# A transformer block on one core: transposes moved to DMA, full-array matmuls at both ends, and a new split of work between ScalarE and VectorE

## The chip, the core and the metric

The kernel runs on one core of one Trainium2 chip. The metric is the device time of one execution in microseconds (us). The core has a matrix engine (TensorE, "PE" in the profile, with its weight loads as "PEld"), VectorE ("DVE"), ScalarE ("ACT"), GpSimd ("POOL") and SyncE ("SP"), which here issues all DMA transfers. Each engine works through its own list of instructions in order and waits on semaphores for the others.

## The reference

2048 rows of width 640 go through layer normalization, attention with 32 heads of width 20, a residual add, a second normalization and a gated feed-forward block of width 1728 with a second residual add. Inputs and output are bf16.

```
xn = (x - mean) / sqrt(var + 1e-5)
q, k, v = split(xn @ wqkv)                      # 32 heads of 20
p = softmax(q @ k.T / sqrt(20));  o = p @ v     # per head, 2048 x 2048
h = x + o @ wo
hn = layernorm(h)
out = h + (gelu(hn @ w_gate) * (hn @ w_up)) @ w_down
```

## The kernel before, in words

**Order of work.** The kernel doesn't issue instructions as it goes. `Sched.op` (line 59) records every operation with an engine, an estimated duration, a latency, a priority, what it reads and writes and which PSUM banks it takes. `Sched.schedule` (92) then simulates all engines with these estimates and writes down an order for each; `emit` (229) puts it out with semaphore waits. So the order on every engine, SP included, is fixed by the planner's estimates: where something takes longer on the chip than planned, everything behind it in that engine's list waits too. Priorities run from P_QK (0, the attention scores) over P_PV (1) and P_EPI (2) to P_BG (3, background). Where the planner sees TensorE idle for too long it adds a filler matmul (`idle`, 1031).

**Prologue** (574 on). For each 128-row tile of x: statistics on VectorE (`ln_stats`, 499: two bn_stats and an aggregation), one reciprocal square root for four tiles (`ln_rsqrt`, 509), the normalization itself on ScalarE or VectorE (`ln_apply`, list LNE), five TensorE transposes into PSUM and one copy of the result to SBUF (`transposes`, 549; the list LNV names the engine of that copy). GpSimd meanwhile clears two padded weight arrays and copies the weights into them with each head padded from 20 to 32 rows (`pad`, 486).

**Projections** (`proj`, 598). Eight groups of four heads. Keys and queries of a group are 128 x 512 blocks. Beside each, the squares are summed by a second matmul: keys give the maximum squared norm (`kmx`, `khalf`), and half of the sum of norms is put into an extra row of the query as a softmax shift. All 128-column matmuls outside of attention are issued as four matmuls of 32 columns (`quarters`, 587), each on its own quarter of the array.

**Attention.** Queries come in seven chunks of 512, 512, 256, 256, 256, 128 and 128 rows (`CHUNKS`), divided into 32 slots of 64 tiles; a tile is 128 keys by 512 columns of scores. The string PATS says for each slot whether units (`unit`, 727) have three and two tiles in turn, or always three. A unit's scores are written to adjacent PSUM banks, and ScalarE takes the exponential of the whole unit at once. In some three-tile units the third tile goes to VectorE, which computes a polynomial exponential (`d_exp`, 695): one pass out of PSUM for each tile and then seven passes over a pair of tiles. The string DS gives the number of pairs in each slot, 95 pairs or 190 tiles in all. The normalized output of a slot is put into `o_nat` by `epilogue` (837).

**After a chunk** (`post`, 870). Each row tile of `o_nat` is transposed (five blocks, `transposes`), multiplied by `wo`, added to a reloaded x, normalized, transposed again, and goes through gate, gelu, up, multiply and down. This is background work that runs beside the attention of the next chunk. For the last chunk (`tail`) there is nothing beside it but what is left of the chunk before.

The planner gives DMA loads a landing time from a formula (line 206).

Of the kernel before, what the change touches and what calls it, by code (L numbers as in the profile page):

```python
# [6 lines left out]
ALU = mybir.AluOpType  # L7
# [11 lines left out]
DMA_RATE = 0.36  # L19
LATE = (0, 1, 2, 3, 4)  # L20
LNE = [{'a': 'act', 'd': 'dve'}[x] for x in 'aaaaaaaadddddddd']
LNV = [{'a': 'act', 'd': 'dve'}[x] for x in 'aaaaaaaaaaaaaaaa']
# [6 lines left out]
MODE_SWITCH = {"pe": 0.1, "act": 1.3}  # L29
# [14 lines left out]
class Op:  # L44
    __slots__ = ("i", "eng", "fns", "dur", "lat", "prio", "deps", "succ", "nd", "ready",
                 "acq", "rel", "group", "sem", "tag", "mode", "start", "fin", "pos", "know", "mb")


class Sched:
# [9 lines left out]
    def op(self, eng, fns, dur, prio, reads=(), writes=(), acq=(), rel=(), after=(), sem=None, lat=None, mode=None, mb=0.0):  # L59
# [4 lines left out]
        o.mb = mb  # L64
        o.tag = writes[0] if writes else None
# [26 lines left out]
    def schedule(self):  # L92
# [20 lines left out]
        dma_free = 0.0  # L113
        qk_left = sum(o.eng == "pe" and o.prio[0] == P_QK for o in ops)
        t = 0.0
        while done < len(ops):
# [4 lines left out]
            for e in ENGINES:  # L121
# [103 lines left out]
                qk_left -= e == "pe" and o.prio[0] == P_QK  # L225
# [74 lines left out]
_cs = (512, 512, 256, 256, 256, 128, 128)  # L300
# [13 lines left out]
ND, NDA = 4, 6  # L314
RSQRT_MAGIC = float(0x5F3759DF)

P_QK, P_PV, P_EPI, P_BG = 0, 1, 2, 3


def bass_sequential_preLN__mha_block__glu_gated_geglu__prompt_kernel(  # L320
# [12 lines left out]
    with ExitStack() as es:  # L333
# [22 lines left out]
        gq = sb("gq", [128, 128])  # L356
# [74 lines left out]
        zb = carve(2 * 512).rearrange("p (i s) -> p i s", i=2)  # L431

# [18 lines left out]
        cst(I("memset", gq[:], 0.0), "gq")  # L451
        for j in range(4):
            cst(I("memset", gq[32 * j:32 * j + 21, 32 * j:32 * j + 1], 1.0), "gq", 1)
        cst(I("memset", wk_pad, 0.0), "wkpm", 2600)
        cst(I("memset", wq_pad, 0.0), "wqpm", 2600)
# [29 lines left out]

        def pad(dst, off, h0, h1, mkey, key, a0, a1):
            src = wqk[:, a0:a1, off + h0 * DH:off + h1 * DH].rearrange("p a (h e) -> p a h e", e=DH)
            e_ops.append(op(POOL, I("tensor_copy", dst[:, a0:a1, h0:h1, 1:21], src),
                            0.1 + (a1 - a0) * (h1 - h0) * DH * 0.0012, P_BG, reads=["wqk", mkey], writes=[key, "pool"]))
# [4 lines left out]
        for dst, off, key in pads:  # L494
            for a in range(NA):
                pad(dst, off, 4, 32, key + "m", key, a, a + 1)


        def ln_stats(src, t, rkeys, prio, after=()):
# [7 lines left out]
            return [a, b]  # L507

# [40 lines left out]
        def transposes(src, rkeys, dst, wkey, banks, prio, evac, after=()):  # L549
            bk = Bank(*banks)  # L550
            key = ("bk", id(bk), sc_id())
            for a in range(NA):
                op("pe", lambda eng, a=a: eng.transpose(  # L553
                    bank16(bk, D)[:, 128 * a:128 * a + 128], src[:, a * 128:(a + 1) * 128], ident[:]),
                   0.056, prio, mode="full", reads=list(rkeys) + ["ident"], writes=[key], acq=[bk] if a == 0 else [],
                   after=tuple(sc.rd.get(wkey, ())) if a == 0 else ())
            v = lambda: bank16(bk, D).rearrange("p (a e) -> p a e", a=NA)
            if evac == "act":
                op("act", lambda eng: eng.activation(dst, v(), ACT.Copy), c_act(D), prio, reads=[key],
                   writes=[wkey], rel=[bk], after=after)  # L560
            else:
                op("dve", lambda eng: eng.tensor_copy(dst, v()), c_dve(D), prio, reads=[key], writes=[wkey],
# [11 lines left out]
        for t0 in range(0, NT, 4):  # L574
            for t in range(t0, t0 + 4):
                ln_stats(x_sb[:, t, :], t, [f"x{t // 4}"], P_EPI)
# [7 lines left out]

        w_readers = []

# [5 lines left out]
        def chain(bk, key, n, steps, reads, prio, acq=True, after=()):  # L592
            for k, (l, r) in enumerate(steps):
                yield op("pe", quarters(lambda: bank(bk, n), l, r, k == 0, k == len(steps) - 1),
                    c_mm(n), prio, mode="col", reads=reads, writes=[key], acq=[bk] if (k == 0 and acq) else [],
                    after=after if k == 0 else ())

        def proj(which, g, c, banks, prio, evac="dve"):
# [28 lines left out]
            gm = gq if which == "k" else gqh  # L627
# [67 lines left out]
        def d_exp(b, tile, prio):  # L695
# [3 lines left out]
            if not first and d_n[1] == 0:  # L699
                d_n[:] = [0, 1]  # L700
# [10 lines left out]
            if h == 0:  # L711
                return
# [356 lines left out]
```

## Time and profile before

| what | value |
|---|---|
| median of 3 runs | 963.77 us (963.38 to 965.76) |
| profiled execution | 966.23 us, span 964.4 us |
| mean granted TensorE clock | 0.996 |
| VectorE busy | 769.8 us (80%) |
| ScalarE busy | 913.5 us (95%) |
| first exponential starts | 38.67 us into the span |
| last exponentials end | about 924.6 us |

Times in the profile count from the span's start. In a group's row, the columns are the line, engine, operation, output <- input with shapes, count, then total busy us and mean ns of one, then the idle time of the engine just before such instructions and what ended it. The line is often 341, a helper that builds most instructions, so groups are told apart by their tiles. In a row of the timeline, the columns are start, length, engine, line, operation and count, and in brackets the idle time before it. In the chain of waits each piece has a start, a length, an engine and a tile.

### The profile page before, as it was taken

To read this page: it belongs to the slowest core of one execution; us is meant where nothing else is said; L and a number is where in the kernel's file an instruction comes from. 1 tells how busy PE (TensorE), PEld (TensorE's weight loads), DVE (VectorE), ACT (ScalarE), POOL (GpSimd) and SP (SyncE) were. 2 spreads that over 40 slices of the span, in tenths; PEclk is the share of its full clock that TensorE was granted. 3 is DMA by queue.
4 is the path that set the end of the run, shared out by engine and by line. 5 is a ranking of instruction groups with operands and counts; after the bars stand their busy time and mean duration, and the time that the engine had idled before them with its cause. 6 is when DMAs were issued, how large, how long until landed. Compare 5 with 4: busy or idle time off the path is not lost.

```text
span 964.4 us, 35452 instructions
## 1 busy us (share of the span) xinstructions
PE 896.8 (93%) x16302; PEld 395.0 (41%) x16302; DVE 769.8 (80%) x1644; ACT 913.5 (95%) x872; POOL 19.9 (2%) x42
## 2 busy tenths in 40 slices
PE   5999999999999999899999999999999999899976
PEld 3533332222332332323343333444554455566655
DVE  8658857998988788699778888889889877988451
ACT  5799999999999999999999999999999999999961
POOL 8000000000000000000000000000000000000000
PEclk9999999999999999999999999999999999999999
DMA  7000000000000520000010000010000000000000
GB/s 246 3 30 1 2 2 1 2 1 1 2 1 1 211 68 1 2 1 9 16 36 2 2 2 2 9 30 23 2 3 10 23 3 17 17 3 4 12 10 18
DMA packets 11764, 20.04 MB, mean 21 GB/s; under 512 B 544, under 2 KB 9696, under 8 KB 11616
## 3 DMA queue, kind: packets, MB, share of 16 engines
q1 hardware_dynamic: 11616, 17.78, 5.5%
q8 instruction: 128, 2.10, 0.9%
q14 instruction: 20, 0.16, 0.1%
HBM read 15.16 MB, written 2.62 MB: 18 GB/s over the span
## 4 chain that ended last, share of the span: by engine, by line
ACT 75%; PE 16%; DVE 7%; DMA 1%; issue 1%; DVEq 0%
ACT pts L341 44%; ACT rege L341 30%; PE ps L589 9%; PE ps L341 6%; DVE qt_all L341 2%; DVE rege L341 2%; DVE stats L341 1%; DMA rege<-in_A_x_dram 1%; ACT L341 1%; PE ps L553 1%; DVE mv L341 0%; PE ps L850 0%; DVE rege L971 0%; DVE rege L959 0%; DVE osb L341 0%
## 5 line engine op out<-in xcount | busy, mean ns | idle before, releaser
L341 ACT ACTIVATE pts<-ps 128x1024 bf16<-128x1024 f32 (+1 forms) x491 | 560.4, 1352 | 7.9 <-PE ps L341 7.6
L341 ACT ACTIVATE rege<-ps 128x1024 bf16<-128x1024 f32 (+1 forms) x307 | 365.6, 1351 | 0.2
L341 PE MATMUL ps<-qt_all,kt_all 32*128 32x256 bf16 (+2 forms) x3584 | 312.9, 288 | 32.5 <-ACT pts L341 12.9
L341 PEld LDWEIGHTS ps<-qt_all,kt_all 32*128 32x128 bf16 x3584 | 97.6, 92 | 276.8 <-ACT pts L341 126.1
L589 PE MATMUL ps<-rege,regw 128*32 128x256 bf16 (+2 forms) x3780 | 173.2, 289 | 14.3 <-issue 8.2
L341 PE MATMUL ps<-pts,v_all 128*21 128x256 bf16 (+2 forms) x1998 | 162.4, 292 | 1.7 <-DVE osb L341 0.9
L589 PE MATMUL ps<-regw 128*32 128x512 bf16 (+1 forms) x1920 | 133.9, 354 | 1.4 <-DVE qt_all L640 0.8
L341 PE MATMUL ps<-rege,v_all 128*21 128x256 bf16 (+2 forms) x1438 | 129.2, 292 | 0.1
L589 PEld LDWEIGHTS ps<-rege,regw 128*32 128x32 bf16 x3780 | 85.0, 96 | 46.6 <-issue 24.2
L341 DVE TENSOR_TENSOR rege<-rege 128x1024 bf16<-128x1024 bf16 (+1 forms) x149 | 101.6, 684 | 1.5
L589 PE MATMUL ps<-regw,rege 128*32 128x320 bf16 (+1 forms) x1792 | 94.4, 305 | 1.7 <-DVE rege L971 0.7
L341 DVE TENSOR_SCALAR rege<-ps 128x512 int16<-128x512 f32 x114 | 77.9, 684 | 18.1 <-PE ps L341 17.7
L341 DVE TENSOR_SCALAR rege<-rege 128x1024 int16<-128x1024 int16 (+1 forms) x206 | 84.5, 419 | 2.0
L341 PEld LDWEIGHTS ps<-pts,v_all 128*21 128x21 bf16 x1998 | 48.1, 90 | 64.7 <-issue 55.4
L341 DVE TENSOR_TENSOR qt_all<-qt_all 128x1024 bf16<-128x1024 bf16 (+1 forms) x97 | 66.3, 683 | 1.0
L589 PEld LDWEIGHTS ps<-regw 128*32 128x32 bf16 x1920 | 45.8, 95 | 40.3 <-issue 14.4
L341 DVE TENSOR_SCALAR qt_all<-ps 128x512 int16<-128x512 f32 x76 | 52.1, 686 | 12.2 <-PE ps L341 11.6
L341 DVE TENSOR_SCALAR qt_all<-qt_all 128x1024 bf16<-128x1024 int16 (+1 forms) x135 | 56.2, 420 | 1.5
L341 PEld LDWEIGHTS ps<-rege,v_all 128*21 128x21 bf16 x1438 | 40.2, 90 | 39.1 <-issue 33.9
L589 PEld LDWEIGHTS ps<-regw,rege 128*32 128x32 bf16 (+1 forms) x1792 | 44.6, 96 | 27.7 <-issue 15.0
L341 PE MATMUL ps<-wo,gq 128*21 128x256 bf16 x331 | 55.1, 273 | 0.0
L971 DVE TENSOR_TENSOR rege<-rege,ps 128x512 bf16<-128x512 bf16 (+2 forms) x53 | 35.9, 678 | 16.7 <-PE ps L589 16.5
(82 smaller groups left out, 690.4 us busy)
## 6 DMA issues: line engine op xcount, KB each, us to landing
rege<-in_A_x_dram SPq DMA_DIRECT2D x6, 640.0 KB, 5.8
out_dram<-rege SPq DMA_DIRECT2D x16, 160.0 KB, 1.8
regw<-in_B_w_gate_dram SPq DMA_DIRECT2D x1, 2160.0 KB, 8.7
regw<-in_B_w_up_dram SPq DMA_DIRECT2D x1, 2160.0 KB, 14.1
regw<-in_B_w_down_dram SPq DMA_DIRECT2D x1, 2080.0 KB, 19.3
rege<-in_A_wqkv_dram SPq DMA_DIRECT2D x1, 1600.0 KB, 11.3
rege<-in_A_x_dram SPq DMA_DIRECT2D x3, 320.0 KB, 3.4
regw<-in_A_wqkv_dram SPq DMA_DIRECT2D x1, 800.0 KB, 12.9
```

The source lines that it names most:

```text
L341: return lambda eng: getattr(eng, method)(*args, **kwargs)
L553: op("pe", lambda eng, a=a: eng.transpose(bank16(bk, D)[:, 128 * a:128 * a + 128], src[:, a * 128:(a + 1) * 128], ident[:]), 0.056, prio, ...
L589: return [lambda eng, j=j: eng.matmul(out()[j:j + 32], l[:, j:j + 32], r, start=start, stop=stop, tile_position=(0, j), skip_group_check=T ...
L971: hdone.append(op("dve", lambda eng, bu=bu, fv=fv, m=m, w_=w_: eng.tensor_tensor(fv, fv, bank(bu, w_)[0:m, :], ALU.mult), c_dve(w_), p, re ...
```

## The change

- **Transposes.** In `post` of all chunks but the last, both transposes of a row tile become five DMAs each (`dma_start(..., transpose=True)`) issued by SP from SBUF to SBUF, in place of five TensorE transposes and a VectorE copy. For chunks after the first, a block of `o_nat` waits only for the head groups that it holds. The planner counts 0.06 us of SP and 2.6 us of latency for each. In the last chunk the first two blocks of `o_nat` are transposed apart from the other three, still on TensorE.
- **ScalarE and VectorE tiles.** DS now counts single tiles, 209 in all; a slot with an odd number ends with a half-width pass. PATS has six three-tile slots in place of five. From the third chunk on VectorE has seven buffers in place of four.
- **Prologue.** Statistics of five row tiles (list LNS) are computed on ScalarE by two passes with an accumulated sum. Nine of the sixteen copies after the transposes go to VectorE. GpSimd clears only the pad columns, and copies the weights of head groups 1 to 7 after the normalization. The maximum of the squared key norms is taken over 128 columns (the four heads' sums lie on different partitions and are folded by a small matmul). For the first query block the squared norms are added before the key maximum is known.
- **Full-array matmuls.** An operation can carry an alternative (`alt`). Before the first and after the last attention scores, the planner issues one matmul over the full 128 columns (`whole`) in place of four quarters, in the projections, in `post` and for filler matmuls.
- **Smaller ones.** The epilogue of 128-row chunks does one multiply for its four head groups; the last chunk's down projection starts without the last multiply; the planner's table load for ScalarE is 1.55 in place of 1.3 us.

```diff
-PATS = '22222222322222222222332222322322'
-DS = '02204423321344542244444334433422'
+PATS = '22222222322222232222332222222332'
+DS = '06408656668788988888888688668844'
...
+LNS = [{'a': 'act', 'd': 'dve'}[x] for x in 'ddaadddddddaddaa']
+LNE = [{'a': 'act', 'd': 'dve'}[x] for x in 'aaaaaaaaddaddddd']
+LNV = [{'a': 'act', 'd': 'dve'}[x] for x in 'ddddadaaadaaadad']
...
+                if o.alt is not None and (not qk_left or not qk_done):
+                    o.fns, o.mode = o.alt, "full"
...
-        cst(I("memset", wk_pad, 0.0), "wkpm", 2600)
-        cst(I("memset", wq_pad, 0.0), "wqpm", 2600)
+        for w_, key in ((wk_pad, "wkpm"), (wq_pad, "wqpm")):
+            v_ = w_.rearrange("p a h e -> p (a h) e")
+            cst(I("memset", v_[:, :, 0:1], 0.0), key, 160)
+            cst(I("memset", v_[:, :, 21:32], 0.0), key, 1760)
...
+        def ln_stats_act(src, t, rkeys, prio):
+            op("act", I("activation", xn_t[:, t % 2, :], src, ACT.Identity, scale=1.0 / D, accum_out=mv[:, t, 0:1]), 0.65, prio,
+               reads=rkeys, writes=[("mv0", t), ("xnj", t % 2)])
+            op("act", I("activation", xn_t[:, t % 2, :], src, ACT.Square, bias=mv[:, t, 0:1], scale=-1.0, accum_out=mv[:, t, 1:2]),
+               0.65, prio, reads=list(rkeys) + [("mv0", t)], writes=[("mv1", t), ("xnj", t % 2)])
...
+            if DT and dma:
+                aft = tuple(after) + tuple(sc.rd.get(wkey, ()))
+                for a in range(NA):
+                    op("sp", I("dma_start", dst[:, a, :], src[:, a * 128:(a + 1) * 128], transpose=True), 0.06, prio,
+                       reads=rkeys if len(rkeys) < NG or first_ else rkeys[0:(a * 128 + 127) // 80 + 1], writes=[wkey] if a == NA - 1 else [(wkey, a)], sem=f"t{wkey[1]}", lat=2.6, after=aft)
+                return
...
+        def whole(out, l, r, start, stop):
+            return [lambda eng: eng.matmul(out()[0:l.shape[-1]], l, r, start=start, stop=stop, skip_group_check=True)]
...
-                op("dve", lambda eng: eng.tensor_reduce(kmx[:, g, c:c + 1], bank(b2), AX.X, ALU.max), c_dve(512), prio,
+                op("dve", lambda eng: eng.tensor_reduce(kmx[:, g, c:c + 1], bank(b2, 128), AX.X, ALU.max), c_dve(128), prio,
...
-            n = 2 * int(DS[s_])
+            n = int(DS[s_], 16)
...
-                transposes(o_nat[:, tt, :], [("on", g) for g in range(NG)], oT[:, :, ht * 128:(ht + 1) * 128],
-                           ("hnT", ht), banks, P_EPI, ev, after=first)
+                if tail:
+                    transposes(o_nat[:, tt, :], [("on", g) for g in range(4)], oT[:, :, ht * 128:(ht + 1) * 128],
+                               ("oTa", ht), banks, P_EPI, "dve", after=tuple(sc.rd.get(("hnT", ht), ())), al=(0, 1))
+                    transposes(o_nat[:, tt, :], [("on", g) for g in range(NG)], oT[:, :, ht * 128:(ht + 1) * 128],
+                               ("hnT", ht), banks, P_EPI, ev, after=first, al=(2, 3, 4))
+                else:
+                    transposes(o_nat[:, tt, :], [("on", g) for g in range(NG)], oT[:, :, ht * 128:(ht + 1) * 128],
+                               ("hnT", ht), banks, P_EPI, "dve", after=first, dma=True, first_=c == 0)
...
-                           banks, p, ev, after=first)
+                           banks, p, "dve", after=first, dma=not tail)
...
-                           writes=[key], acq=[bk] if f == 0 else [], after=hdone[-2:] if f == 0 else ())
+                           writes=[key], acq=[bk] if f == 0 else [], after=hdone[-4 if tail else -2:][:2] if f == 0 else ())
```

More of the change, by code (lines that the diff above doesn't have):

```diff
@@ L693, in bass_sequential_preLN__mha_block__glu_gated_geglu__prompt_kernel, with d_exp @@
         p_next = [0]
[L695 to L700 removed]
+        def d_exp(b, tile, prio, end):
+            c = slots[tile[0]][0]
+            first = c == 0
+            nd, dvs, dfs, nm_ = ((NDA, dva, dfwa, "a"), (ND, dv, dfw, "b"), (NDC, dvc, dfw, "b"))[min(c, 2)]
+            if d_n[1] != min(c, 2):
+                d_n[:] = [0, min(c, 2)]
             i, h = (d_n[0] // 2) % nd, d_n[0] % 2
```

174 lines of the change are left out of this document (117 added, 57 removed).

## The prediction

> **What bounds the kernel now.** I read the head of the page first, then a table of stages cut where ScalarE's stream of exponentials begins and ends, then the chain of waits.
>
> ```profile
> span 964.4 us, 35452 instructions
> PE 896.8 (93%) x16302; PEld 395.0 (41%) x16302; DVE 769.8 (80%) x1644; ACT 913.5 (95%) x872; POOL 19.9 (2%) x42
> ```
>
> ```profile
> 0.00:38.67 38.67, 28.65 (x444) 17.01 (x444) 31.45 (x98) 22.51 (x36) 19.87 (x42) 1.00 0.45 154
> ...
> 257.30:475.00 217.70, 205.90 (x2526) 68.69 (x2527) 187.04 (x379) 217.64 (x208) 0.00 (x0) 1.00 0.10 34
> 475.00:592.00 117.00, 110.44 (x1869) 45.53 (x1861) 93.03 (x196) 115.05 (x111) 0.00 (x0) 0.99 0.04 11
> ...
> 924.60:964.40 39.80, 27.68 (x1127) 21.17 (x1127) 11.17 (x28) 9.63 (x13) 0.00 (x0) 0.96 0.04 12
> ```
>
> The columns are the stretch, its length, then busy PE, PEld, DVE, ACT, POOL. There are three kernels in one: a prologue of 38.7 us in which no engine is full, 885.9 us of attention in which ScalarE is full (217.64 of 217.70 in query chunk 1), and a tail of 39.8 us with ScalarE almost idle. Each needs its own sum. ScalarE's price of a tile is read from the chain, where its exponentials stand end to end:
>
> ```profile
> 60.42 2.26 ACT rege L341 x2
> ...
> 155.53 2.75 ACT rege L341 x3
> ```
>
> ```profile
> L341 ACT ACTIVATE pts<-ps 128x1024 bf16<-128x1024 f32 x328 | 353.8, 1211 | 0.2
> L341 ACT ACTIVATE pts<-ps 128x1536 bf16<-128x1536 f32 x162 | 263.8, 1641 | 7.7 <-PE ps L341 7.6
> L341 ACT ACTIVATE rege<-ps 128x1024 bf16<-128x1024 f32 x206 | 226.5, 1206 | 0.2
> L341 ACT ACTIVATE rege<-ps 128x1536 bf16<-128x1536 f32 x101 | 163.1, 1647 | 0.0
> ```
>
> Three two-tile exponentials take 2.75 us, so one is 0.917; one of each kind takes 2.26, so a three-tile one is 1.343. (The means of 1211 and 1641 ns overlap their neighbours and are not the price.) Now 534 x 0.917 + 263 x 1.343, and one single tile, make 843.4 us of the 885.9.
>
> **The change, part by part: ScalarE.** Running the two lists PATS and DS through the lines that form units gives 543 two-tile and 251 three-tile exponentials, with 209 tiles on VectorE instead of 190: 543 x 0.917 + 251 x 1.343 = 835.0. That is **-8.4 us**, of it 3.6 in chunk 1 (8 tiles more) and 3.5 in chunk 2 (8 more), as long as nobody makes ScalarE wait.
>
> **VectorE** must carry those tiles.
>
> ```profile
> L341 DVE TENSOR_SCALAR rege<-ps 128x512 int16<-128x512 f32 x114 | 77.9, 684 | 18.1 <-PE ps L341 17.7
> ...
> L631 DVE TENSOR_REDUCE kmx<-ps 128x1 f32<-128x512 f32 x32 | 21.7, 687 | 13.1 <-PE ps L589 13.0
> ...
> L562 DVE COPY rege<-ps 128x640 bf16<-128x640 bf16 x30 | 14.4, 487 | 5.5 <-PE ps L553 5.1
> ```
>
> ```profile
> 436.64 1.20 DVE qt_all L341 x2
> ...
> 442.49 0.33 DVE qt_all L341
> ```
>
> End to end a PSUM read or a bf16 product costs 0.60 and a scalar pass 0.33, so a tile is 0.60 plus half of (4 x 0.33 + 3 x 0.60), 2.2 us. Eight tiles are 17.4. The 30 evacuations of line 562 go (0.49 each, 8 of them per large chunk, 3.9). Chunk 1 becomes 187.0 + 17.4 - 3.9 = 200.5 of 214.1 us, chunk 2 93.0 + 17.4 - 3.9 = 106.5 of 113.5: both 94%. It fits, with little air. The key maxima shrink from 512 to 128 columns, in chunk 0, which has room; the small fold that they need instead is cheaper still. The merged epilogue multiply for the 128-row chunks and the half-width last pair are worth fractions of a microsecond and lie in the same cover; I count them as nothing, and at 94% their loss would cost at most their own time, under 1 us.
>
> **Transposing DMAs.** 15 row tiles x 2 transposes x 5 blocks are 150 PE transposes removed and 150 DMAs put on SP, which issues in order. TensorE's saving is worth nothing in attention, where filler matmuls take its idle time. What counts is lateness: every engine's order is written from a plan, and the plan gives a block 0.06 us of SP and 2.6 us to land, so five land 2.9 us after the first. If they land later, the matmul that reads them blocks TensorE's queue, the scores behind it, and then ScalarE. The trace shows this once already:
>
> ```profile
> 490.44 6.01 DMA rege<-in_A_x_dram
> ```
>
> ```profile
> 499.13 1.45 ACT L341 ACTIVATE pts<-ps 128x1536 bf16<-128x1536 f32 x1 [1.85 <-PE ps L341]
> ```
>
> A reload planned at 4.1 us by the plan's own formula (0.64/0.36 + 1.9 + 0.6 x 0.64) took 6.01, and ScalarE stood still for 1.85 us: lateness passes through almost whole. No transposing DMA is in the trace; the nearest rows are small plain ones.
>
> ```profile
> 750.79 0.39 SPq L341 DMA_DIRECT2D rege<-in_A_x_dram  x1
> 751.22 0.47 SPq L341 DMA_DIRECT2D out_dram<-rege  x1
> ```
>
> ```profile
> out_dram<-rege SPq DMA_DIRECT2D x16, 160.0 KB, 1.8
> ...
> rege<-in_A_x_dram SPq DMA_DIRECT2D x2, 160.0 KB, 2.5
> ```
>
> Let a block take c us of SP or of the queue. The fifth lands at 4c + 1.8, which is 4c - 1.1 beyond the plan. This hurts before the gate matmuls, which wait for the last tile of a chunk, once in each of chunks 0 to 5. Where a chunk has several tiles, each tile's 5c also has to keep up with normalized rows that come about 1.8 us apart (my estimate from chunk 0, four between 337.7 and 343.1): nine tiles come after the first of their chunk, 5c - 1.8 each. The output-side transposes hurt less: all but their last block depend on earlier head groups alone and go out early, except in chunk 0, where the q projections stand between. So the cost is 6 x (4c - 1.1) + 9 x (5c - 1.8). At c = 0.39 it is 4, at 0.47 it is 8, at 0.30 under 2. I take **+8** (c = 0.47, the store). Below nothing it can hardly go: the path that it replaces is hidden, and its freed VectorE time is counted above. SP is also passed by reloads and stores in the same order; a store that waits for its second half holds the transposes behind it, but the next chunk's chain starts later than that store, so I add nothing for it.
>
> The Trainium skill has a price for the operation itself, in "VectorE: DVE Perf Modes", section "The three transpose paths": 1309 ns for a 128x128 bf16 block by the DMA crossbar against 390 ns on TensorE. No run here shows it. Used for c, it would make this term 67 us and the whole change a loss of some 44 us.
>
> **Prologue.**
>
> ```profile
> 2.40 8.80 POOL L341 MEMSET regw<- 128x5120 bf16 x2
> ...
> 9.34 1.89 DVE L341 CAST mv<-mv 128x8 bf16<-128x8 f32 x1
> ...
> 26.59 1.51 DVE L341 TENSOR_SCALAR rege<-rege,mu,rs 128x640 bf16<-128x640 bf16 x4
> ...
> 28.66 2.49 ACT L559 ACTIVATE regw<-ps 128x640 bf16<-128x640 bf16 x4
> ...
> 37.26 0.75 DVE L640 SCALAR_TENSOR_TENSOR qt_all<-ps,khalf,qt_all 128x512 bf16<-128x512 f32 x1
> ...
> 38.67 2.37 ACT L341 ACTIVATE pts<-ps 128x1536 bf16<-128x1536 f32 x2 [3.78 <-PE ps L341]
> 42.24 1.45 ACT L341 ACTIVATE pts<-ps 128x1536 bf16<-128x1536 f32 x1 [1.21 <-PE ps L341]
> ```
>
> ```profile
> L341 DVE BATCH_NORM_STATS2 stats<-rege 128x6 f32<-128x320 bf16 x64 | 28.3, 475 | 1.7 <-DMA rege<-in_A_x_dram 1.4
> ```
>
> VectorE's normalization ends at 28.1 and sets the first exponential. Five tiles' statistics leave it (10 x 0.44 = 4.4). The long cast, which ends as GpSimd's two memsets end (11.2), loses 1.7, since only the pad columns are cleared now. Some seven of the nine evacuations that ScalarE hands over (0.49 each, 3.4) come before the last normalization. Net -2.7. Behind it, four evacuations in a row on ScalarE (2.49) become two on each engine, -1.2; the reduction 0.69 to 0.2 and the final add 0.75 to 0.3, with the squared-norm matmul taken ahead of the maximum, against four small new steps of about 0.15: about -1. ScalarE gets ten passes of about 0.62, mostly in the time before 11.5 in which it had nothing. The ten pad copies for the later head groups, moved behind the normalization, now run beside the key chain. Sum **-5**, between -1 (copies slow the chain) and -8.
>
> **Tail.**
>
> ```profile
> 927.64 0.85 PE L589 MATMUL ps<-rege,regw 128*32 128x128 bf16 x48 [0.63 <-ACT rege L341]
> 928.43 0.45 PE L553 MATMUL ps<-ident,o_nat 128*128 128x128 bf16 x5
> ...
> 935.15 1.02 PE L589 MATMUL ps<-rege,regw 128*32 128x128 bf16 x51 [1.44 <-issue]
> ...
> 943.16 3.20 PE L589 MATMUL ps<-rege,regw 128*32 128x128 bf16 x216
> 947.52 1.97 PE L589 MATMUL ps<-rege,regw 128*32 128x128 bf16 x128 [1.16 <-issue]
> 951.54 1.97 PE L589 MATMUL ps<-rege,regw 128*32 128x128 bf16 x128 [2.05 <-issue]
> 955.29 1.41 PE L589 MATMUL ps<-rege,regw 128*32 128x128 bf16 x68 [1.78 <-issue]
> 957.31 4.32 PE L589 MATMUL ps<-regw,rege 128*32 128x320 bf16 x112 [0.61 <-DVE rege L948]
> ```
>
> ```profile
> 29.16 0.73 PE L553 MATMUL ps<-ident,rege 128*128 128x128 bf16 x10
> ```
>
> Here TensorE stops after bursts of 128 quarter matmuls for about 2 us with nothing that it waits for ("issue"): it seems to run out of instructions. 32 products of 128x128 by 128 columns take 955.29 - 951.54 = 3.75 us, 0.117 each. As one full-array matmul a product costs what a transpose of that size does, (0.73 - 0.45)/5 = 0.056. The last chunk's gate and up (140 products, 943.16 to 956.7 = 13.5 us) become 140 x 0.056 = 8, **-5.5**. Chunk 5's 70 up products, 927.64 to 936.2, become 4, so the last chunk's statistics no longer stand behind their VectorE multiplies, and its down products fit before the gate: of the 18.6 us from 924.6 to 943.16 I let go **-4**. The down products start before the last multiply (0.6, so **-0.5**). Together **-10**; from -5 (only the stalls of the last gate and up go) to -13.
>
> **Sum.** -8.4 - 5 - 10 + 8 = -15.4. The profiled execution took 966.2 us (span 964.4), 2.5 above the median of the three runs, 963.8; carried to the median the forecast is **948**.
>
> **Rivals.** *Everything lands in time* (c at 0.3 or less, or slack that I don't see): the 8 vanish, 940. For it speaks that TensorE has waits of its own to lend; against it, the 1.85 us above. *Transposes too slow, the other sign*: the place is the gate matmul of chunks 0 to 5; the price is the formula; gains of 23.4 are used up at c = 0.67. At c = 0.85 the cost is 36 and the time 976. Against it: plain issues of 0.39 and 0.47; for it: no row shows that a transpose is as cheap as a copy. The page of the Trainium skill named above stands at the far end of this rival. *VectorE becomes the bound in chunks 1 and 2*: if half of the idle 30.7 and 24.0 us there are waits that can't be filled, chunk 1 needs 216 us and chunk 2 118.5, together 7 more: 955.
>
> **How the numbers follow.** Chances: forecast 0.48 (its own range 943 to 956), all in time 0.24, VectorE the bound 0.08, transposes too slow 0.20. A difference of 0.3% (3 us) is about what a measurement can tell. Slower gets the last case, 0.20; within 0.3% gets 0.05 out of the slow end of the others; faster 0.75. The range goes from 936 (all in time, prologue and tail at their better ends) to 976, the slow case at c = 0.85; beyond lies about half of that case and a little below.
>
> **What would show it.** Right: ScalarE at full in attention with exponentials of 835 us; first exponential near 33 to 35; no "issue" gaps of 2 us in the tail, gate and up in 8 to 9 us, tail near 30. In the list of DMAs, transposes with a landing of some 2 to 4 us; at the gate matmuls of each chunk, TensorE waiting for them a microsecond or two, and ScalarE behind it. Wrong: SP busy for 0.7 us or more per block, ScalarE waiting tens of microseconds, or VectorE at 97% and more in chunks 1 and 2.

## The result, and the profile after

The changed kernel takes **1045.07 us** (median of 4 runs, 1044.04 to 1046.15) where the kernel before takes 963.58 beside it: a ratio of 1.0841, with a 95% interval of 1.0817 to 1.0865. The forecast was 948, with 976 as the upper end. It is 81.5 us slower where some 15 us faster were expected.

The head of the page of the changed kernel, with the strips of ScalarE and of TensorE's granted clock:

```profile
span 1043.3 us, 33388 instructions
PE 895.1 (86%) x15135; PEld 387.1 (37%) x15138; DVE 783.8 (75%) x1705; ACT 913.3 (88%) x880; POOL 17.4 (2%) x54
...
ACT  8799999999989579999895799959869799859991
PEclk9999999999989789999997899979979899979999
```

ScalarE and TensorE have as much to do as before (913.5 and 896.8 us there), VectorE 14 us more. But ScalarE's share fell from 95% to 88%, and within attention its strip is down to between 5 and 8 in a dozen slices; the clock's strip falls at most of the same places. The stages say where the time lies. This is the same table of stretches as in the prediction (stretch, length, busy PE, PEld, DVE, ACT, POOL, then the clock), cut at the first and the last exponential:

```profile
0.00:36.22 36.22, 21.58 (x174) 12.44 (x177) 28.28 (x95) 26.73 (x48) 17.39 (x54) 1.00 0.48 164
36.22:1013.66 977.44, 848.34 (x14642) 354.66 (x14641) 744.20 (x1585) 877.85 (x820) 0.00 (x0) 0.94 0.07 19
1013.66:1043.30 29.64, 25.19 (x320) 20.02 (x320) 11.33 (x27) 8.71 (x12) 0.00 (x0) 1.00 0.04 13
```

Against the kernel before (38.67, 885.9 and 39.8 us), the prologue is 2.5 shorter, the tail 10.2 shorter, and attention 91.5 longer. The same cut of attention before:

```profile
38.67:924.58 885.91, 840.48 (x14732) 356.82 (x14731) 727.17 (x1518) 881.35 (x824) 0.00 (x0) 1.00 0.05 15
```

ScalarE was busy for 881.35 of 885.91 there; here it is for 877.85 of 977.44. So ScalarE's own work shrank by 3.5, and its idle time grew from 4.6 to 99.6. That idle time is what has to be explained. In the list of ScalarE's instructions in order of time, these are two of the exponentials that it was late for (start, duration, and in brackets the idle time before it):

```profile
359.05 1.02 ACT L353 ACTIVATE rege<-ps 128x1024 bf16<-128x1024 f32 x1 [9.45 <-PE ps L353]
370.69 1.02 ACT L353 ACTIVATE pts<-ps 128x1024 bf16<-128x1024 f32 x1 [7.84 <-PE ps L353]
```

Both wait for scores from TensorE, at a time when the first chunk's rows are normalized; at 568 and 580 us, with the next chunk's, stand two more of 9.21 and 8.83. What TensorE and VectorE wait for is in the table of waits (us in total, times, longest):

```profile
ACT pts L353 <- PE ps L353: 62.6, 26, 11.3
...
PE ps L636 <- DMA rege<-xn_t: 43.5, 5, 10.9
ACT rege L353 <- PE ps L353: 40.3, 14, 10.9
...
DVE xn_t L353 <- DMA rege<-xn_t: 20.3, 4, 6.0
```

Nearly all of ScalarE's idle time is waiting for scores (62.6 and 40.3 over the whole run). Line 636 is the helper that issues quarter matmuls; those that wait for the transposed normalized rows are the feed-forward's gate matmuls: 43.5 us in only five waits, one in each of chunks 0 to 4, with the scores of line 353 queued behind them. VectorE waits 20.3 us in four waits before it may write normalized rows. The chain of waits of the stretch from 340 to 380 us, which holds the two late exponentials (start, duration, what), shows both ("SPq" is SP's queue, "issue" time in which nothing that the profile shows was waited for):

```profile
343.04 0.28 DVE xn_t L353
...
352.97 1.23 SPq L353
354.20 0.04 issue
354.24 2.42 DMA rege<-xn_t
...
356.69 0.45 DVE xn_t L353
357.13 1.21 DVE qt_all L353 x2
...
358.39 3.41 PE ps L353 x15
...
366.99 2.37 DMA rege<-xn_t
...
369.49 0.62 PE ps L636 x3
```

Between 343 and 366 us the rows of SP alternate like the two shown: a transposing DMA holds it for 1.23 us, with 0.04 to the next, **1.27 us a block**, and the data is there 2.4 us after its issue began. Twenty of them stand one behind the other here (the list of SP's instructions; start, duration, count):

```profile
259.82 26.66 SPq L353 DMA_TRANSPOSE rege<-o_nat  x20
...
342.90 25.32 SPq L353 DMA_TRANSPOSE rege<-xn_t  x20
```

The two late exponentials are now readable. VectorE finished the normalized rows of the second tile at 343.3. `xn_t` has two buffers (its index is `t % 2`), so the third tile may be written only once the first has been transposed out of its buffer, and the fourth only once the second has. VectorE's list shows both waits:

```profile
350.23 0.45 DVE L353 TENSOR_SCALAR xn_t<-rege,mu,rs 128x640 bf16<-128x640 bf16 x1 [4.29 <-DMA rege<-xn_t]
...
356.69 0.45 DVE L353 TENSOR_SCALAR xn_t<-rege,mu,rs 128x640 bf16<-128x640 bf16 x1 [5.68 <-DMA rege<-xn_t]
```

The second tile's last block lands at 356.66. VectorE can't go on in its list until then, the query evacuations `qt_all` that stand behind it start at 357.13, the scores that need them at 358.39, and ScalarE gets its exponential at 359.05, 9.45 us late. Then the last tile's blocks land at 369.36, the gate matmul of line 636 starts at 369.49 with scores behind it, and ScalarE is late again by 7.84.

### The profile page after: what moved, and what is told of

Read it like the earlier page. It is cut to its first block, busy times and chain, and to the rows that moved or that the text cites. A ratio compares the mean times of both kernels' runs of the same rounds, so it can differ in the third digit from the quotient of the medians.

```text
span 1043.3 us, 33388 instructions
## 1 busy us (share of the span) xinstructions
PE 895.1 (86%) x15135; PEld 387.1 (37%) x15138; DVE 783.8 (75%) x1705; ACT 913.3 (88%) x880; POOL 17.4 (2%) x54
## 4 chain that ended last, share of the span: by engine, by line
ACT 60%; PE 21%; SPq 8%; DVE 7%; DMA 4%; issue 1%; DVEq 0%
ACT pts L353 34%; ACT rege L353 24%; PE ps L353 9%; PE ps L636 8%; SPq L353 8%; DVE rege L353 2%; PE ps L632 2%; DVE qt_all L353 2%; DMA rege<-xn_t 2%; DMA rege<-in_A_x_dram 1%; ACT L353 1%; DMA rege<-o_nat 1%; PE ps L922 1%; ACT xn_t L353 0%; DVE xn_t L353 0%
## 5 line engine op out<-in xcount | busy, mean ns | idle before, releaser
L353 ACT ACTIVATE pts<-ps 128x1024 bf16<-128x1024 f32 (+1 forms) x487 | 551.0, 1307 | 63.1 <-PE ps L353 62.6
L353 ACT ACTIVATE rege<-ps 128x1024 bf16<-128x1024 f32 (+1 forms) x307 | 356.6, 1295 | 40.7 <-PE ps L353 40.3
L636 PE MATMUL ps<-rege,regw 128*32 128x256 bf16 (+2 forms) x2916 | 165.4, 320 | 53.4 <-DMA rege<-xn_t 43.5
L636 PE MATMUL ps<-regw 128*32 128x512 bf16 (+1 forms) x1668 | 121.5, 361 | 1.3 <-DVE qt_all L667 0.6
L636 PEld LDWEIGHTS ps<-rege,regw 128*32 128x32 bf16 x2916 | 74.2, 98 | 89.2 <-issue 54.4
L353 DVE TENSOR_TENSOR rege<-rege 128x1024 bf16<-128x1024 bf16 (+2 forms) x156 | 105.0, 673 | 1.4
L353 DVE TENSOR_SCALAR qt_all<-ps 128x512 int16<-128x512 f32 x109 | 74.7, 685 | 28.7 <-PE ps L353 28.0
L353 DVE TENSOR_SCALAR rege<-rege 128x1024 bf16<-128x1024 int16 (+2 forms) x207 | 83.7, 413 | 1.4
L636 PE MATMUL ps<-regw,rege 128*32 128x320 bf16 (+1 forms) x1568 | 84.6, 308 | 0.0
L353 DVE TENSOR_TENSOR qt_all<-qt_all 128x1024 bf16<-128x1024 bf16 (+3 forms) x118 | 79.8, 676 | 1.1
L1046 DVE CAST rege<-ps 128x512 bf16<-128x512 f32 (+2 forms) x53 | 36.0, 680 | 50.1 <-PE ps L636 46.5
L353 DVE TENSOR_SCALAR qt_all<-qt_all 128x1024 bf16<-128x1024 int16 (+2 forms) x173 | 70.9, 416 | 1.9
L353 PE MATMUL ps<-wo,gk 128*21 128x256 bf16 x344 | 62.1, 278 | 0.0
L636 PEld LDWEIGHTS ps<-regw,rege 128*32 128x32 bf16 (+1 forms) x1568 | 38.7, 97 | 24.5 <-issue 13.5
```

The source lines that it names most:

```text
L353: return lambda eng: getattr(eng, method)(*args, **kwargs)
L636: return [lambda eng, j=j: eng.matmul(out()[j:j + 32], l[:, j:j + 32], r, start=start, stop=stop, tile_position=(0, j), skip_group_check=T ...
L1046: cp.append(op("dve", lambda eng, bg=bg, fv=fv, m=m, w_=w_: eng.tensor_copy(fv, bank(bg, w_)[0:m, :]), c_dve(w_), pre, reads=[kg], writes= ...
```

## The experiments

Each ratio is to the kernel before, run on the same chip beside it.

**Is it the transposing DMAs, and at which end?** Four runs put them in or take them out. The first is the change with all transposes left on TensorE, everything else as changed.

```diff
-DT = 1
+DT = 0
```

> The changed kernel with all transposes back on TensorE and VectorE, everything else as changed. Theory A (the whole loss is the transposing DMAs; the rest of the change is a gain): ScalarE's idle of 100 us in attention goes, prologue 36.2 us and tail 29.6 us stay as in the changed kernel, so 963.6 - 8.4 (exponentials) - 2.5 (prologue) - 10.1 (tail) = 943, up to 950 if VectorE is tight. Rival V (209 tiles overload VectorE once the evacuations are back on it): 955 to 975, with ScalarE waiting in chunks 1 and 2.

Measured: 958.53 us, ratio 0.9951 (0.9935 to 0.9967). The DMAs cost 86.5 us (1045.07 - 958.53), more than the whole loss; the rest of the change gains 4.3 us over the kernel before (962.82 beside it), less than the 943 to 950 of my theory, and the time lies just inside what the rival of a full VectorE gave (955 to 975). The table of stretches for it, attention and tail:

```profile
36.18:908.39 872.21, 821.17 (x14086) 345.10 (x14085) 740.09 (x1598) 866.26 (x816) 0.00 (x0) 1.00 0.05 15
908.39:956.90 48.51, 45.17 (x515) 35.43 (x513) 21.38 (x43) 13.17 (x15) 0.00 (x0) 1.00 0.05 15
```

ScalarE is idle for 6.0 us in attention, so VectorE makes it wait no more than before (4.6), and attention is 13.7 us shorter. But the tail has grown to 48.5, where the changed kernel's is 29.6. That is taken up again below.

The next two keep one of the two uses of the DMA.

```diff
-                               ("hnT", ht), banks, P_EPI, "dve", after=first, dma=True, first_=c == 0)
+                               ("hnT", ht), banks, P_EPI, "dve", after=first, dma=False, first_=c == 0)
```

> The changed kernel with only the transposes of the normalized rows by DMA; those of the attention output are back on TensorE. Adding up ScalarE's waits in the changed kernel by place, about 70 of the 100 us stand where normalized rows are transposed (349 to 376, 568 to 584, 763 to 768, 832 to 836, 928 to 942 us): 943 + 70 = 1013, between 1000 and 1025. If the two kinds cost by count (75 each), 993.

Measured: 1030.21 us, ratio 1.0695 (1.0668 to 1.0721), 5 us above the expected range.

```diff
-                           banks, p, "dve", after=first, dma=not tail)
+                           banks, p, "dve", after=first, dma=False)
```

> The changed kernel with only the transposes of the attention output by DMA; those of the normalized rows are back on TensorE. By place, about 25 of the 100 us (289 to 297, 513 to 515, 690 to 698, 897 to 900 us): 943 + 25 = 968, between 955 and 980. If the two kinds cost by count, 993.

Measured: 975.22 us, ratio 1.0124 (1.0089 to 1.0159). Against the run without DMAs, the normalized rows cost 71.7 us and the attention output 16.7; the sum of 88.4 is close to the whole loss of 86.5. Attention alone grows by 71.6 us (872.2 to 943.8) and 18.1 (to 890.3), and by 105.2 with both (to 977.4), so 15.5 in attention come only when both stand in one queue; the tail, 48 us in both of these runs and 29.6 with both DMAs, pays that back. The order of work is fixed before the run, so this is the plan's doing: with both kinds by DMA it has the feed-forward's last activation of 2048 columns on ScalarE at 966.19, ahead of the last exponential (1013.66), and in the runs with one kind behind it (983.08 after 980.25, and 929.46 after 926.64).

The other direction: the kernel before with nothing but the DMAs added (its `transposes` gets the same branch).

```diff
-        def transposes(src, rkeys, dst, wkey, banks, prio, evac, after=()):
+        def transposes(src, rkeys, dst, wkey, banks, prio, evac, after=(), dma=False, first_=False):
+            if dma:
+                aft = tuple(after) + tuple(sc.rd.get(wkey, ()))
+                for a in range(NA):
+                    op("sp", I("dma_start", dst[:, a, :], src[:, a * 128:(a + 1) * 128], transpose=True), 0.06, prio,
...
+                return
...
-                           ("hnT", ht), banks, P_EPI, ev, after=first)
+                           ("hnT", ht), banks, P_EPI, ev, after=first, dma=not tail, first_=c == 0)
...
-                           banks, p, ev, after=first)
+                           banks, p, ev, after=first, dma=not tail)
```

> The kernel before with one part of the change alone: the transposing DMAs in all chunks but the last, with the plan's 0.06 and 2.6 us. Theory A (SP needs 1.27 us for each block, so five blocks land 4 to 5 us after the plan, and TensorE, VectorE and then ScalarE stand): the same loss as in the changed kernel against its sibling with TensorE transposes, 1045 - 958.5 = 86.5, so 963 + 87 = 1050, between 1030 and 1070. Rival (the loss comes from DMA transposes together with VectorE's fuller load): 963 + 30 to 50.

Measured: 1062.29 us, ratio 1.1017 (1.0998 to 1.1036), with ScalarE idle for 96.5 us of attention (889.55 busy of 986.09). In its table of waits stands the same wait of the feed-forward matmuls, which have line 595 here, as in the changed kernel:

```profile
PE ps L595 <- DMA rege<-xn_t: 39.9, 5, 12.0
```

So the DMAs alone are enough for the harm (98.7 us here), and it does not need VectorE's added tiles.

**Is it the time that a DMA takes, or the place in the order that its wrong price gave it?** All engines' orders are written from a plan, and the plan holds a block for 0.06 us of SP and 2.6 us of landing. Here the plan is given what the trace shows, both numbers at once; the work is the same, but the planner may place other fillers (33626 instructions against 33388).

```diff
-                    op("sp", I("dma_start", dst[:, a, :], src[:, a * 128:(a + 1) * 128], transpose=True), 0.06, prio,
-                       reads=rkeys if len(rkeys) < NG or first_ else rkeys[0:(a * 128 + 127) // 80 + 1], writes=[wkey] if a == NA - 1 else [(wkey, a)], sem=f"t{wkey[1]}", lat=2.6, after=aft)
+                    op("sp", I("dma_start", dst[:, a, :], src[:, a * 128:(a + 1) * 128], transpose=True), 1.27, prio,
+                       reads=rkeys if len(rkeys) < NG or first_ else rkeys[0:(a * 128 + 127) // 80 + 1], writes=[wkey] if a == NA - 1 else [(wkey, a)], sem=f"t{wkey[1]}", lat=1.2, after=aft)
```

> The changed kernel with the transposing DMAs kept, and only the planner's numbers for them made to fit the trace: 1.27 us of SP for each and 1.2 us more to land, in place of 0.06 and 2.6. Theory A (the loss is not the transfer but the order written from a wrong price): TensorE no longer stands before work that is late, so the loss shrinks from 100 us to under 15: 943 to 960. Rival B (SP's time and the small buffers cannot be hidden by any order): 1000 to 1045.

Measured: 986.58 us, ratio 1.0243 (1.0223 to 1.0263): between the two theories. 58 of the 86.5 us are gone. Of the 42.3 us that ScalarE still idles in attention in the profiled execution of 991.45 us (878.80 busy of 921.08), one wait makes half:

```profile
693.41 1.94 ACT L353 ACTIVATE rege<-ps 128x1024 bf16<-128x1024 f32 x2 [21.72 <-PE ps L353]
```

The chain of waits ahead of it:

```profile
686.94 1.23 SPq L353
...
688.22 2.04 DMA out_dram<-rege
...
690.28 0.50 DVE rege L1074
...
690.88 1.94 PE ps L922 x8
```

From 671.8 to 688.2 SP is at ten transposes of the attention output, with one reload among them; the last transpose is the first row. Behind them in its queue stands a plain store of an earlier chunk's result; VectorE's next write into the stored buffer (line 1074) waits for the store to land, and TensorE's matmul behind that. The prediction had named this queue ("a store that waits for its second half holds the transposes behind it") and added nothing for it; what it overlooked is the other order, transposes that hold a store.

The same honest plan with the tile lists of the kernel before (190 tiles on VectorE rather than 209):

```diff
-        PATS = '22222222322222232222332222222332'
-        DS = '06408656668788988888888688668844'
+        PATS = '22222222322222222222332222322322'
+        DS = '04408846642688a84488888668866844'
```

> Transposing DMAs with the plan's numbers corrected (1.27 and 1.2 us), and the old lists (190 tiles). Theory C: VectorE keeps air, the background work stays in its chunks, and the transposes are hidden: 951 to 965. If SP, which issues in order, is what delays (stores and reloads queued behind transposes, as in the 21.7 us wait at 693 us of the run with 209 tiles): 970 to 990.

Measured: **957.21 us**, ratio 0.9927 (0.9911 to 0.9944). Its attention:

```profile
36.38:923.67 887.29, 834.17 (x14627) 353.03 (x14627) 704.36 (x1487) 882.43 (x824) 0.00 (x0) 1.00 0.08 21
```

All 150 DMAs are still there, at a median of 1.23 us of SP each, and ScalarE idles for 4.9 us, as in the kernel before (4.6). The wait of the gate matmuls, 43.5 us in the changed kernel, is gone from the table of waits:

```profile
PE ps L636 <- DMA rege<-xn_t: 0.3, 1, 0.3
```

TensorE's clock is 1.00 again where it was 0.94: its falls came with the stalls, not with the DMAs. To complete the square, the wrong price with these lists, so with the diff of the lists alone:

> The changed kernel with the old lists (190 tiles) and the wrong price in the plan (0.06 and 2.6 us). Theory A (the wrong price is the loss, whatever VectorE does): 1030 to 1055. If the fuller VectorE were needed for the loss: 957 to 990.

Measured: 1048.99 us, ratio 1.0896 (1.0876 to 1.0916).

| price of a block in the plan | 209 tiles | 190 tiles |
|---|---|---|
| 0.06 us, landing 2.6 | 1045.1 | 1049.0 |
| 1.27 us, landing 1.2 | 986.6 | 957.2 |

With the wrong price the lists hardly matter; with the right one the transposes are hidden at 190 tiles and not at 209. So most of the loss is one of order, and with 190 tiles all of it: the same transfers, planned at their length, stall nothing there. With 209 tiles 28 us are left (986.58 against 958.53); half of ScalarE's idle time in that run is the one wait behind a store, and what the fuller VectorE adds to the rest was not separated.

**Is SP's time per byte or per instruction?** The honest plan with 190 tiles, each block moved as two DMAs of 64 rows.

```diff
+                    for h in range(2):
+                        op("sp", I("dma_start", dst[:, a, 64 * h:64 * h + 64], src[64 * h:64 * h + 64, a * 128:(a + 1) * 128], transpose=True), 1.27, prio,
```

> Corrected plan and old lists, but each transposing DMA cut into two of 64 rows by 128 columns, each planned at 1.27 us of SP. If SP's time goes by the instruction, each half still takes 1.23 us and a tile 12.7 us; if it goes by size, a half takes about 0.62 us and a tile 6.4 as before. The total time is of less interest: 957 to 985.

Measured in one run: 1047.59 us, far above the 957 to 985 expected. In its list of SP's instructions:

```profile
259.60 54.72 SPq L353 DMA_TRANSPOSE rege<-o_nat  x40
...
340.77 42.60 SPq L353 DMA_TRANSPOSE rege<-xn_t  x32
```

That is 1.37 and 1.33 us for half a block, so the time goes by the instruction and not by the bytes. Twice the time of SP is no longer hidden, though the plan counts 1.27 for each half: ScalarE is idle again for some 80 us of attention, and half of that is a single wait:

```profile
738.13 1.94 ACT L353 ACTIVATE pts<-ps 128x1024 bf16<-128x1024 f32 x2 [42.69 <-PE ps L353]
```

The chain ahead of it is the one of 693 us again: 20 transposes and a reload on SP up to 732.8, a store behind them, VectorE's write into the stored buffer, TensorE. So a length that is nearly right in the plan is not enough by itself; why the planned order stalls at this store stays open.

**What is left without the DMAs?** The run with transposes on TensorE came out at 958.5, some 10 us above what the prologue, exponentials and tail promised. The time is in the order of the feed-forward. Its large activations on ScalarE (2048 columns) are a mark of where that stands; first the kernel before, chunk 1:

```profile
570.80 6.55 ACT L341 ACTIVATE rege<-rege 128x2048 bf16<-128x2048 bf16 x5
```

and the change with transposes on TensorE, chunk 1 and a later one:

```profile
627.67 6.55 ACT L353 ACTIVATE rege<-rege 128x2048 bf16<-128x2048 bf16 x5
...
911.21 3.28 ACT L353 ACTIVATE rege<-rege 128x2048 bf16<-128x2048 bf16 x2
```

Chunk 1's comes 57 us later than before, and one chunk's comes after the last exponential (ends at 908.4), so that feed-forward that should hide under attention is left for the tail. My reading was that 19 more tiles on VectorE do this: ScalarE does not wait, but VectorE's share of the feed-forward, which has the lowest priority in the plan, falls behind. The test is the same kernel with the 190 tiles of before.

```diff
-DT = 1
+DT = 0
...
-        PATS = '22222222322222232222332222222332'
-        DS = '06408656668788988888888688668844'
+        PATS = '22222222322222222222332222322322'
+        DS = '04408846642688a84488888668866844'
```

> All transposes on TensorE, the rest of the change kept, but the old lists for units and VectorE tiles (190). Theory C (with 209 tiles and the evacuations VectorE has no time for the background work of chunks 1 to 4, so feed-forward work of chunk 4 slides into the tail, and the gain of 14 us in attention comes back as 19 us of tail): with 190 tiles the tail is that of the changed kernel, 30 us, attention is that of the kernel before, 886, and the prologue 36: span 952, time about 951, faster than with 209 tiles by 7. Rival (fewer tiles on ScalarE always help): 958.5 + 8 = 966.

Measured: 955.30 us, ratio 0.9907 (0.9893 to 0.9922), 4 us above the 951 expected and far from the rival's 966. With fewer tiles taken off ScalarE it is faster. Attention is back at 886.4 us and the tail at 30.5, and the late chunk's activation is ahead of the last exponential again:

```profile
878.49 3.28 ACT L353 ACTIVATE rege<-rege 128x2048 bf16<-128x2048 bf16 x2
```

Beside the run of 957.21 it also gives the value of the DMAs when they are planned at their length: 955.3 with the transposes on TensorE against 957.2 by DMA, the intervals of the two ratios overlapping. They gain nothing; planned at 0.06 us with these lists they cost 93.7 (1048.99 - 955.30).

**What are full-array matmuls in the tail worth?** The last run with all products after the last scores as quarters again, the feed-forward's above all.

```diff
-                if o.alt is not None and (not qk_left or not qk_done):
+                if o.alt is not None and not qk_done:
```

> As the run with TensorE transposes and 190 tiles, but with full-array matmuls only before the first scores; after the last scores quarters again. The tail should lose what the prediction gave to full-array matmuls there: 8 to 10 us more than its sibling, with gaps of 1 to 2 us in which TensorE waits for nothing that shows. If the tail is bound by the chain of dependences and not by TensorE's instructions: 0 to 3 us more.

Measured: 962.55 us, ratio 0.9989 (0.9976 to 1.0002): +7.2 us, of 8 to 10 expected. TensorE's instructions in its tail show the pauses again:

```profile
939.31 3.19 PE L636 MATMUL ps<-rege,regw 128*32 128x128 bf16 x213
944.27 1.97 PE L636 MATMUL ps<-rege,regw 128*32 128x128 bf16 x128 [1.77 <-issue]
...
951.49 1.36 PE L636 MATMUL ps<-rege,regw 128*32 128x128 bf16 x68 [1.50 <-issue]
```

The same 140 products in the changed kernel:

```profile
1027.98 8.33 PE L632 MATMUL ps<-rege,regw 128*128 128x128 bf16 x140
```

13.5 us (939.31 to 952.85) against 8.33. The whole run is 7.2 us longer for it, and that is most of the 8.3 us that the kernel with 190 tiles gains over the one before, with attention as long as before.

**Can both gains be had?** Two runs with lists between the two, the first with the DMAs in the honest plan (198 tiles), the second with the transposes on TensorE (201).

```diff
-        PATS = '22222222322222232222332222222332'
-        DS = '06408656668788988888888688668844'
+        PATS = '22222222322222222222332222322222'
+        DS = '13408855662888a84588888658886846'
```

> Transposing DMAs with the corrected plan (1.27 and 1.2 us), and lists for units and VectorE tiles chosen anew for that plan (198 tiles, added where VectorE has air). Eight tiles fewer on ScalarE are worth 3.4 us, and a background that ends earlier some more: 949 to 955 against 957 with the old lists. If the freed VectorE time is not the limit: 957.

Measured: 959.23 us, ratio 0.9975 (0.995 to 0.9999), from 954.93 to 968.41 over 12 runs; a miss. ScalarE idles for 11.3 us of attention: 8 tiles more than in the run of 957.21 give nothing beside the DMAs.

```diff
-DT = 1
+DT = 0
...
-        PATS = '22222222322222232222332222222332'
-        DS = '06408656668788988888888688668844'
+        PATS = '22222222322222222222332222322322'
+        DS = '26408845744688a84588898668896736'
```

> All transposes on TensorE, lists chosen anew for that (201 tiles): 947 to 953 against 955 with the old lists. If the transposing DMAs are worth anything once they are planned at their price, they beat this run, by up to the 13 us of VectorE time that they free and no less than nothing; if the two come out within 3 us, the DMAs are worth nothing here at any price.

Measured: **947.61 us**, ratio 0.9843 (0.983 to 0.9856), the fastest of all. Its attention and tail:

```profile
36.58:916.25 879.67, 834.70 (x14799) 355.61 (x14798) 737.33 (x1593) 877.26 (x824) 0.00 (x0) 1.00 0.05 15
916.25:945.70 29.45, 24.87 (x328) 20.01 (x328) 11.30 (x26) 8.71 (x12) 0.00 (x0) 1.00 0.04 13
```

Attention is 6.2 us shorter than before, with ScalarE idle for 2.4, and the tail keeps its 29.5: 11 more tiles than before, in another distribution over the chunks, give their gain and the feed-forward stays ahead of the last exponential. It is 9.6 us faster than the best run with DMAs (957.21): with lists chosen for each, the transposes on TensorE are better, so the DMAs are not worth having here at either price.

## Why the prediction was wrong

**The step that failed is "Transposing DMAs", in its price c = 0.47 us for a block.** The runs show 1.27. The mechanism was the one described: the plan's 0.06 us, lateness at the gate matmuls of line 636, TensorE's queue blocked, scores and ScalarE behind it. The formula comes close too: with 1.27 it gives 6 x (4 x 1.27 - 1.1) + 9 x (5 x 1.27 - 1.8) = 64.8 us, and the run with normalized rows alone lost 71.6 in attention. For chunk 0 it gives 17.6, and the two late exponentials shown above waited 17.3; all seven long waits of this kind in the changed kernel (those four, and 10.87, 7.16 and 11.28 in chunks 2 to 4) make 64.6. Only chunk 5, in the formula with 4, shows none. The choice of the end was wrong: plain DMAs of 0.39 and 0.47 were taken as the row nearest to an operation that is another one. The sentence on the Trainium skill ("VectorE: DVE Perf Modes", section "The three transpose paths", 1309 ns for a 128x128 block) stood against it, and the trace now agrees with it: 1.27 to 1.33 us (25.32/20, 26.66/20). With c = 1.27 the working would have said a loss of 41 us, some 1005. Two of the prediction's own sums are off as well, which changes nothing here: at c = 0.47 the formula gives 9.6 and not 8, so the forecast would be 950, and the low end of the range (prologue -8, tail -13) is 934 and not 936.

**The other 40 us of attention (105.2 - 64.8) are terms that the step left out.** Output-side transposes "hurt less" and got nothing; alone they cost 18.1 in attention (16.7 of the whole). Both together cost 15.5 in attention beyond their sum, presumably since ten blocks of a tile then stand in one queue instead of five; no run shows this by itself. The formula itself is 7 short for the normalized rows: its landing of 1.8 us was 2.4, six times 0.6, and it knows only TensorE's wait and not VectorE's, which stood at the two buffers of `xn_t` for 20.3 us. The loss over the whole is 86.5 and not 105.2, because the tail gives 18.9 us back (48.5 to 29.6). TensorE's clock, 0.94 in attention, came with the stalls; how much of the 105 us it adds was not separated.

**Rival "transposes too slow"** was the one that happened, with a chance of 0.20; its place and its mechanism hold. Its end (c = 0.85, 976) was set far too near, at no row. Its point of decision (0.67 us) was too far as well: it set the price against gains of 23.4. The prologue (2.5), the tail (10.2) and ScalarE's own work in attention (3.5) of the changed kernel make some 16, and the run with the transposes on TensorE gained only 4.3. By the formula, 16 are used up at c = 0.57 and 4.3 at c = 0.39, the price of the cheaper plain row (an estimate; no run has a transpose at such a price). The range should have gone on to the price that the prediction itself had cited.

**ScalarE -8.4**: with transposes on TensorE, attention became 13.7 us shorter, but only as feed-forward left it for the tail. Where that stays in (947.61 us, 201 tiles), it is -6.2.

**VectorE "fits, with little air"**: no wait of ScalarE for it, as forecast, and so not the mechanism of the rival; but the load was too full all the same. The 94% was not reached (in the run without DMAs VectorE is busy for some 91% of chunk 1 and 89% of chunk 2): the work with the lowest priority moved on to later chunks, and the last of it behind the last exponential, 8.7 us of tail more than before in the run without DMAs. The 958.5 us of that run are close to the rival's 955, for another reason; the agreement is luck.

**Prologue -5**: -2.5, the first exponential at 36.22 against 38.67. ScalarE's share of the statistics is dearer than 0.62 a pass. (A slip besides: LNV gives eight of the sixteen copies to VectorE, not nine.) Three of its instructions, in order of time:

```profile
6.70 0.81 ACT L353 ACTIVATE xn_t<-rege,mv 128x640 bf16<-128x640 bf16 x1
7.42 0.19 ACT L353 ACTIVATION_READ_ACCUMULATOR xn_t<-rege,mv 128x1 f32 x1
...
9.69 1.28 ACT L353 ACT_TABLE_LOAD   x1
```

A pass takes 0.73 to 0.81 us (the means of its two forms) and the reading of its sum another 0.19, and a table load of 1.28 falls between. Three rows place the loss: VectorE's last normalizations (before: 26.59, in the prediction), and the last block of keys out of PSUM, first the kernel before, then the changed one.

```profile
25.51 1.51 DVE L353 TENSOR_SCALAR rege<-rege,mu,rs 128x640 bf16<-128x640 bf16 x4
```

```profile
32.90 0.69 ACT L610 ACTIVATE kt_all<-ps,e 128x512 bf16<-128x512 f32 x1 [1.07 <-PE ps L589]
```

```profile
29.84 0.69 ACT L657 ACTIVATE kt_all<-ps,e 128x512 bf16<-128x512 f32 x1 [0.42 <-PE ps L632]
```

The normalization ends 1.1 us earlier, where -2.7 was forecast. From there to the last keys it is 2.0 shorter (-1.2 forecast), and from the keys to the first exponential 0.6 longer (5.69 against 5.08), where about -1 was forecast. So the first and the last of the three terms failed; no run takes apart which of their small steps it was.

**Tail -10**: -10.2 (39.8 to 29.6), the 140 products in 8.33 us where 8 were forecast, and no pause of 2 us in them. This step was right in size. The run with quarters shows the cause for 7.2 us of it; the remaining 3, from the smaller changes of the tail, no run tests.

**The sum by stages**: prologue -2.5, attention without DMAs -13.7, DMAs +105.2, tail -10.2, together +78.8; the spans differ by 78.9, and the medians by 81.5.

## What to carry to other kernels

Where every engine's order is written from a price list, an operation with a wrong price stalls all of them, and the loss says little about the operation: with 190 tiles on VectorE the same 150 transfers cost 93.7 us planned at 0.06 us and 1.9 at 1.27, so measure a new operation by itself before anything is ordered around it. The right price is not always enough: with 209 tiles 28 us of 86.5 were left at 1.27, and one wait of 21.7 us in that run stood behind a store in the same queue. Do not bound an operation that the trace lacks by a cheaper relative of it; where the two ends lie far apart and the sign hangs on the choice, the range has to hold both. An engine that can carry more work on average still delays what has the lowest priority on it, so look for that work in the tail.

## What the runs showed of the hardware

A transposing DMA of 128x128 between SBUF buffers held its issuing queue for 1.23 us in the changed kernel (median of each kind, up to 2.4), with 0.04 to the next, and landed 2.4 us after its issue began, where the plain DMAs that stand alone in the changed kernel's list were issued in 0.33 to 0.58; with half the rows it took 1.33 to 1.37 with the pause, so halving it saved nothing. A product of 128x128 by 128 columns as one full-array matmul took 0.0595 us (8.33/140), and as four quarter matmuls 0.097 over the same 140 products (13.5/140), pauses without a wait included. And TensorE's granted clock was 0.94 over an attention full of stalls of some 10 us, down to 0.70 in the stretch from 340 to 380 us, in which it was busy for 22 of 40 us, but 1.00 in the run of 957.21, where the same DMAs stalled nothing. The stretch, in the changed kernel:

```profile
340.00:380.00 40.00, 22.16 (x183) 6.03 (x181) 18.45 (x43) 20.34 (x21) 0.00 (x0) 0.70 0.09 17
```
